# Retention followed by a SoLU layer on one core: another order for the first seven chunks

## The chip, the cores and the metric

The kernel runs on one core of a Trainium2 chip. A core has five engines that run side by side, each with its own queue, in order: PE (matrix multiplication; its weight loads are listed apart as PEld), DVE (vector work), ACT (activation functions and copies with a scale), POOL (a slower vector engine) and SP, which here only issues transfers. The metric is the device time of one execution in microseconds (us), as the median over runs.

## The reference

Two layers follow each other. The first is a retention: scores of queries and keys, scaled, multiplied by a decay that depends on head and distance and is zero above the diagonal, then applied to the values. The second is a dense layer with a softmax in it.

```python
scores = (1 / sqrt(64)) * (q @ k.transpose(0, 1, 3, 2))       # 8 batches, 8 heads, 576 positions, 64 wide
ret = scores * Dmat                                            # gamma[h] ** (i - j) for i >= j, else 0
x = (ret @ v).transpose(0, 2, 1, 3).reshape(4608, 512)
h = x @ w_in                                                   # 512 x 1024
sm = softmax(h)
solu = h * sm
ln = (solu - mean(solu)) / sqrt(var(solu) + 1e-6) * g_ln
out = ln @ w_out                                               # 1024 x 512
```

## The kernel before

The 4608 tokens are cut into 36 chunks of 128. Batches go in pairs: chunk 0 is the first 128 positions of batch 0, chunk 1 those of batch 1, chunk 2 the next 128 of batch 0, and so on through chunk 7; chunk 8 holds the last 64 positions of both. Then the next pair follows. Within a batch a state (keys times values, decayed) is carried from chunk to chunk, so chunk 4 needs the state that chunk 2 has left, and chunk 2 that of chunk 0.

Each chunk passes through a series of small steps, each a function with a name of two letters. In the order of one chunk:

- ld loads q, k and v (three transfers of 256 KB on SP's queue). cq, ck and cv bring them to 16 bits, with the decay factors for q and v.
- tq transposes q and k on PE; eq copies the result out of PSUM (qkT). sc makes the scores on PE; mk multiplies them by the mask on DVE (two instructions).
- kv multiplies keys and values on PE; ad adds the carried state on DVE (t); dk and d3 decay it on POOL in two forms.
- av and fs make the retention's output on PE, from the chunk itself and from the carried state; ex copies it out (xT).
- m1 is the first product of the dense layer, x times w_in (eight matmuls of 512 columns into h); mr is a quarter of it, so that it can start while w_in is still arriving. mx is the row maximum (DVE), xp the exponential (ACT), so the product with h and its sum (DVE), ce the subtraction of the mean (DVE, two instructions), sq the sum of squares (ACT), rt the inverse root (POOL, three instructions).
- tu transposes the result on PE, eu copies it out (uT). m2 is the second product, with w_out (eight matmuls into o). st scales it on ACT and stores it through SP.

Beside these, li loads a quarter of w_in (512 KB) and wi brings half of a quarter to 16 bits; lo loads a quarter of w_out (512 KB) and wo brings an eighth of it to 16 bits with the factor of the norm; wu runs a number of matmuls on a tile of zeros (w), whose result nobody reads; c1 and c2 load and prepare constants. The last letter of a step names its engine where there is a choice: a for ACT, v for DVE, g for POOL.

The order is written out by hand as three strings of such steps, START, LOOP and END, and nothing reorders them: each engine gets its instructions in the order of the string, and each queue its transfers. Waits between engines are set by what is read and written, and by buffers that are used again. `run` (line 612) goes through a string; in LOOP the numbers are relative to the pass, so that pass i makes tu of chunk i-2, so of i-1, m1 and mx of i, kv, ad, av, fs and ex of i+1, tq, eq, sc and mk of i+2 and m2 and st of i-2. START goes as far as pass FIRST, with which the loop begins.

```python
        run(START, 0)
        for i in range(FIRST, NCH - 1):
            run(LOOP, i)
        run(END, NCH - 1)
```

Buffers that matter here: PSUM has four banks of their own for all products but h (tags b0 to b3), and the string BANKS says, allocation by allocation, which of the four is taken; a step that takes a bank waits until what was in it has been read. h has two buffers, released by so. The loads have six buffers of each kind, the 16-bit q, k and v four, uT, u and e three. m2 may not be issued before all eight wo (line 412 ff.).

In START before, SP loads chunk 1, a quarter of w_in, chunk 0, the rest of w_in, chunks 3, 2 and 4, w_out, and then chunks 5 to 9. The first two m2 stand in START, after m1 of chunks 0 to 3, and the loop begins with pass 4.

Of the kernel before, what the change touches and what calls it, by code (L numbers as in the profile page):

```python
# [16 lines left out]

FIRST = 4  # L20
START = """
c1:0 ld:1 li:3 ld:0 ck:0:v li:2 li:1 cq:1:g li:0 cv:1:v ck:1:a cq:0:g wu:0:8 tq:1 ld:3 wu:0:15
kv:1 wi:2:0:v wi:0:0:a eq:1:v ld:2 tq:0 wi:1:1:g cv:0:v wi:3:1:a wu:0:6 sc:1 eq:0:v wi:3:0:a
mk:1 wu:0:3 sc:0 ld:4 kv:0 wi:1:0:v c2:0 lo:0 ad:1 ck:3:a wu:0:1 av:1 ad:0 lo:3 wi:2:1:a mk:0
cq:3:g fs:1 dk:1 tq:3 ex:1:a dk:0 d3:1 wu:0:2 mr:1:3 cq:2:g eq:3:a d3:0 cv:3:v lo:1 mr:1:2
cv:2:g lo:2 ck:2:a wi:0:1:v av:0 kv:3 mr:1:0 sc:3 fs:0 ld:5 cq:4:g ad:3 tq:2 mr:1:1 mk:3
ex:0:a mr:0:2 mr:0:1 kv:2 av:3 mx:1 eq:2:a sc:2 ad:2 dk:3 d3:3 cv:4:g d3:2 mk:2 mr:0:0 mr:0:3
av:2 fs:3 mx:0 fs:2 xp:1 dk:2 wo:0:g ck:4:a ex:2:a tq:4 wo:4:g so:1 kv:4 wu:0:2 m1:2 xp:0
eq:4:a so:0 ce:0 ld:6 wu:0:1 tu:0 ld:7 cq:5:g ce:1 ld:8 ex:3:a ad:4 wo:7:a wo:6:a wo:3:a
wo:2:v sq:1 sc:4 mx:2 m1:3 tu:1 wo:1:a mk:4 eu:0:v av:4 xp:2 wo:5:a ck:5:g cv:5:v tq:5 fs:4  # L30
eq:5:v sq:0 eu:1:a mx:3 rt:1 m2:0 rt:0 cq:6:g so:2 m2:1 st:0 ex:4:a cq:7:g sc:5 ck:6:v cv:6:g
ce:2 xp:3 ld:9 st:1 mk:5 ck:7:g
"""
LOOP = """
tu:-2 so:-1 tq:2 dk:0 d3:0 eq:2:a eu:-2:a ce:-1 m1:0 kv:1 ad:1 av:1 sc:2 mx:0 sq:-2 mk:2 fs:1
# [6 lines left out]
"""  # L42

BANKS = """
012302210201313202132013203200310210302312032103210231023120312032103213021302310231032103213021
302310231032103213021302310231032103201320130213021032103201320130213021032103201320130213021032
10312031201320132103210312031201320132103210312031201320132013231001
"""


# [25 lines left out]
def kernel(  # L76
# [535 lines left out]
    def run(order, base):  # L612

        for token in order.split():
            name, n, *more = token.split(":")
            n = base + int(n)
            if 0 <= n < NCH:
                step[name](n, *more)

    with tc.manual_schedule():  # L620
# [3 lines that stand above are left out]
# [31 lines left out]
```

## Time and profile before

| | us |
|---|---|
| median of 3 runs (lowest, highest) | 227.18 (226.64, 227.31) |
| the profiled execution | 226.83 |
| its span, from the first to the last instruction | 225.0 |
| PE busy in the span (share) | 211.4 (94%) |
| DVE busy | 196.9 (88%) |
| ACT busy | 190.9 (85%) |
| POOL busy | 163.1 (73%) |
| mean granted PE clock | 0.992 |

The page also cuts the span into 40 slices of 5.6 us each and gives the busy share of each in tenths, where 9 is 90% or more:

```
PE   6778889899999999999999999999999999999982
DVE  0078788999999999999999999999999999999780
ACT  2107689699999999999999999999999999999972
```

A busy share is an average over stages with different limits. The start and the last 20 us are filled less than the middle, and a matmul on zeros counts as busy too, so a digit for PE in the first slices says less than one in the middle. What a change is worth is read from the stage where it lies.

### The profile page before, as it was taken

How to read it: one execution, taken by the hardware profiler on the slowest of the kernel's cores; microseconds unless marked ns; L12 is line 12 of the kernel's file. 1: busy time of each engine (PE TensorE's matmuls, PEld its weight loads, DVE VectorE, ACT ScalarE, POOL GpSimd, SP SyncE). 2: the span in 40 equal slices, each digit the busy share in tenths (PEclk: the TensorE clock that was granted, in tenths of full speed). 3: DMA queues.
4: the chain of work that ended last, by engine and by line, in shares of the span. 5: the costliest groups of instructions: out<-in, count | busy, mean ns of one | idle time of the engine just before them, and what ended most of it. 6: DMA issues, size and time to landing. Idle time of an engine off the chain costs nothing.

```text
span 225.0 us, 5803 instructions
## 1 busy us (share of the span) xinstructions
PE 211.4 (94%) x2158; PEld 119.0 (53%) x2158; DVE 196.9 (88%) x340; ACT 190.9 (85%) x299; POOL 163.1 (73%) x243
## 2 busy tenths in 40 slices
PE   6778889899999999999999999999999999999982
PEld 2334355455555555555555555555555555555542
DVE  0078788999999999999999999999999999999780
ACT  2107689699999999999999999999999999999972
POOL 2128868798776998887758989887759988883231
PEclk9699999999999999999999999999999999999999
DMA  7999899999999986988898968988898963111204
GB/s 161 246 345 219 220 332 205 225 235 265 258 216 247 238 165 150 262 198 196 182 215 183 216 134 207 240 203 183 204 197 195 196 136 105 47 50 47 93 3 143
DMA packets 121085, 42.52 MB, mean 189 GB/s; under 512 B 114656, under 2 KB 115040, under 8 KB 121056
## 3 DMA queue, kind: packets, MB, share of 16 engines
q1 hardware_dynamic: 119424, 41.82, 81.4%
q10 hardware_dynamic: 1632, 0.32, 0.9%
q8 instruction: 17, 0.28, 0.5%
q14 instruction: 12, 0.10, 0.2%
HBM read 32.70 MB, written 9.44 MB: 187 GB/s over the span
## 4 chain that ended last, share of the span: by engine, by line
PE 62%; SPq 11%; DVE 10%; ACT 6%; POOL 4%; DMA 4%; issue 2%; ACTq 0%; POOLq 0%; DVEq 0%
PE h L335 20%; PE o L418 20%; SPq L159 9%; PE lp L404 5%; PE tp L189 5%; DMA qf<-in_q_dram 4%; PE sc L213 4%; PE x L303 3%; PE kp L237 3%; PE x L288 3%; ACT e L351 2%; DVE nm L345 2%; SPq L580 2%; DVE u L360 2%; SPq L590 1%
## 5 line engine op out<-in xcount | busy, mean ns | idle before, releaser
L418 PE MATMUL o<-w_out,uT 128*128 128x512 f16 x280 | 66.0, 379 | 0.4
L335 PE MATMUL h<-w_in,xT 128*128 128x512 f16 x264 | 62.4, 379 | 0.1
L166 POOL TENSOR_TENSOR q<-qf,small 128x512 f16<-128x512 f32 x36 | 37.7, 1048 | 12.4 <-DMA qf<-in_q_dram 12.4
L226 DVE TENSOR_TENSOR ret<-sc,tris 128x512 f16<-128x512 f32 x72 | 46.0, 679 | 0.4 <-PE sc L213 0.4
L351 ACT ACTIVATE e<-h,nm 128x1024 f32<-128x1024 f32 x35 | 39.1, 1117 | 6.6 <-DVE nm L345 6.2
L360 DVE SCALAR_TENSOR_TENSOR u<-h,e 128x1024 f16<-128x1024 f32 x35 | 42.4, 1212 | 1.9 <-ACT e L351 1.8
L345 DVE TENSOR_REDUCE nm<-h 128x1 f32<-128x1024 f32 x35 | 42.5, 1214 | 0.9 <-PE h L323 0.9
L418 PEld LDWEIGHTS <-uT 128*128 128x128 f16 x280 | 26.1, 98 | 26.7 <-ACT uT L150 0.7
L383 ACT ACTIVATE sq<-u 128x1024 f16<-128x1024 f16 x35 | 37.4, 1069 | 0.0
L335 PEld LDWEIGHTS <-xT 128*128 128x128 f16 x264 | 24.4, 98 | 23.9 <-issue 0.3
L150 ACT COPY qkT<-tp 128x1024 f16<-128x1024 f16 x33 | 33.4, 1012 | 2.5 <-PE tp L189 1.3
L264 POOL TENSOR_TENSOR s<-t,small 128x512 f16<-128x512 f32 x32 | 33.6, 1053 | 0.0
L150 ACT COPY uT<-lp 128x1024 f16<-128x1024 f16 x33 | 33.6, 1018 | 0.0
L395 POOL TENSOR_TENSOR w<-w,ss 128x1 f32<-128x1 f32 x36 | 6.8, 190 | 34.3 <-ACT sq L383 34.0
L150 POOL CAST k<-kf 128x512 f16<-128x512 f32 x30 | 30.9, 1029 | 0.1
L166 DVE TENSOR_TENSOR v<-vf,small 128x512 f16<-128x512 f32 x33 | 29.3, 887 | 1.8 <-DMA vf<-in_v_dram 1.8
L426 ACT ACTIVATE o_sb<-o,rs 128x512 f32<-128x512 f32 x35 | 23.7, 680 | 0.5 <-POOL rs L396 0.5
L404 PEld LDWEIGHTS <-u 128*128 128x128 f16 x280 | 18.3, 98 | 10.1 <-DVE u L374 1.7
L404 PE MATMUL lp<-ident,u 128*128 128x128 f16 x280 | 21.4, 219 | 1.3 <-ACT o_sb L426 1.0
L150 ACT CAST xT<-x 128x512 f16<-128x512 f32 x36 | 21.1, 586 | 1.1 <-PE x L303 1.0
L396 POOL TENSOR_TENSOR rs<-w,mhalf 128x1 f32<-128x1 f32 x36 | 19.8, 549 | 2.9
L276 POOL TENSOR_TENSOR s<-t,small 128x256 f32<-128x256 f32 x24 | 20.3, 844 | 0.0
(68 smaller groups left out, 255.5 us busy)
## 6 DMA issues: line engine op xcount, KB each, us to landing
qf<-in_q_dram SPq DMA_DIRECT2D x32, 256.0 KB, 4.0
kf<-in_k_dram SPq DMA_DIRECT2D x32, 256.0 KB, 4.6
vf<-in_v_dram SPq DMA_DIRECT2D x32, 256.0 KB, 4.9
out_dram<-o_sb SPq DMA_DIRECT2D x32, 256.0 KB, 2.3
w_in<-in_moe_w_in_dram SPq DMA_DIRECT2D x4, 512.0 KB, 5.8
w_out<-in_moe_w_out_dram SPq DMA_DIRECT2D x4, 512.0 KB, 6.0
qf<-in_q_dram SPq DMA_DIRECT2D x8, 128.0 KB, 3.3
kf<-in_k_dram SPq DMA_DIRECT2D x8, 128.0 KB, 3.3
```

Of the source, the lines that this page charges most:

```text
L150: (engine.copy if engine is nc.scalar else engine.tensor_copy)(out=out, in_=in_)
L166: engine.tensor_tensor(out=dst, in0=T.pop((key, n)), in1=table.unsqueeze(2).to_broadcast([P, H, D]), op=ALU.mult,)
L226: nc.vector.tensor_tensor(out=r, in0=s, in1=m, op=ALU.mult)
L264: nc.gpsimd.tensor_tensor(out=s16, in0=t.unsqueeze(2).to_broadcast([P, 4, 2, D]), in1=gd.unsqueeze(3).to_broadcast([P, 4, 2, D]), op=ALU.mult,
L335: nc.tensor.matmul(out=h[:, i * 512 : (i + 1) * 512], lhsT=xT[:, d], rhs=w_in16[:, d, i * 512 : (i + 1) * 512], start=d == 0, stop=d == 3,)
L345: nc.vector.tensor_reduce(out=nm, in_=T["h", n], axis=AX.X, op=ALU.max, negate=True)
L351: nc.scalar.activation(out=e, in_=T["h", n], func=ACT.Exp, bias=T.pop(("nm", n)), accum_out=s)
L360: nc.vector.scalar_tensor_tensor(out=u, in0=T.pop(("h", n)), scalar=1.0, in1=T.pop(("e", n)), op0=ALU.mult, op1=ALU.mult, accum_out=su,)
L383: nc.scalar.activation(out=s, in_=T.pop(("v", n)), func=ACT.Square, accum_out=ss)
L404: nc.tensor.transpose(out=lp[:, c], in_=u[:, c * P : (c + 1) * P], identity=ident)
L418: nc.tensor.matmul(out=o, lhsT=uT[:, c], rhs=w_out16[:, c], start=c == 0, stop=c == NF - 1)
L426: nc.scalar.activation(out=o_sb, in_=T.pop(("o", n)), func=ACT.Copy, scale=T.pop(("rs", n)))
```

## The change

The change replaces START, moves FIRST from 4 to 7 and rewrites BANKS to fit; no function and no other line is touched. LOOP and END are the same strings, and the loop begins with pass 7.

- SP loads chunks 1 and 0, then all of w_in, then chunks 4, 2, 3, 5 and 6, then w_out, then chunks 7 and up.
- The first products of chunks 0 to 5 stand ahead of the first m2 in the string, and the exponentials of chunks 0, 1, 2 and 4 too (those of 3 and 5 follow it). The m2 of chunks 0, 1, 4, 3 and 2, in this order, come at the end of START, with m1 of chunk 6 among them.
- Up to pass 7 both orders issue the same steps, but for wu: 38 of its matmuls before, 28 after.
- Some steps change engines. To DVE come cq of chunks 0, 1 and 9, eq of chunks 6 to 8, ex of chunks 0 and 6, and eu of chunks 2 and 3; from DVE go, among others, eq of chunks 0, 1 and 5 and eu of chunk 0 (to ACT) and cv of chunks 3, 5, 7 and 9 (to POOL).
- uT is now made for chunks 0, 1 and 4 before the first m2, and for chunks 2 and 3 after it. The stores of chunks 1 and 0 stand on SP's queue ahead of the load of chunk 10, those of chunks 3 and 4 ahead of chunk 11, that of chunk 2 ahead of chunk 12.

```diff
--- before.py
+++ after.py
@@ -17,19 +17,23 @@
 
 
 
-FIRST = 4
+FIRST = 7
 START = """
-c1:0 ld:1 li:3 ld:0 ck:0:v li:2 li:1 cq:1:g li:0 cv:1:v ck:1:a cq:0:g wu:0:8 tq:1 ld:3 wu:0:15
-kv:1 wi:2:0:v wi:0:0:a eq:1:v ld:2 tq:0 wi:1:1:g cv:0:v wi:3:1:a wu:0:6 sc:1 eq:0:v wi:3:0:a
-mk:1 wu:0:3 sc:0 ld:4 kv:0 wi:1:0:v c2:0 lo:0 ad:1 ck:3:a wu:0:1 av:1 ad:0 lo:3 wi:2:1:a mk:0
-cq:3:g fs:1 dk:1 tq:3 ex:1:a dk:0 d3:1 wu:0:2 mr:1:3 cq:2:g eq:3:a d3:0 cv:3:v lo:1 mr:1:2
-cv:2:g lo:2 ck:2:a wi:0:1:v av:0 kv:3 mr:1:0 sc:3 fs:0 ld:5 cq:4:g ad:3 tq:2 mr:1:1 mk:3
-ex:0:a mr:0:2 mr:0:1 kv:2 av:3 mx:1 eq:2:a sc:2 ad:2 dk:3 d3:3 cv:4:g d3:2 mk:2 mr:0:0 mr:0:3
-av:2 fs:3 mx:0 fs:2 xp:1 dk:2 wo:0:g ck:4:a ex:2:a tq:4 wo:4:g so:1 kv:4 wu:0:2 m1:2 xp:0
-eq:4:a so:0 ce:0 ld:6 wu:0:1 tu:0 ld:7 cq:5:g ce:1 ld:8 ex:3:a ad:4 wo:7:a wo:6:a wo:3:a
-wo:2:v sq:1 sc:4 mx:2 m1:3 tu:1 wo:1:a mk:4 eu:0:v av:4 xp:2 wo:5:a ck:5:g cv:5:v tq:5 fs:4
-eq:5:v sq:0 eu:1:a mx:3 rt:1 m2:0 rt:0 cq:6:g so:2 m2:1 st:0 ex:4:a cq:7:g sc:5 ck:6:v cv:6:g
-ce:2 xp:3 ld:9 st:1 mk:5 ck:7:g
+ld:1 c1:0 wu:0:3 ld:0 wu:0:3 cq:1:v li:2 ck:1:v cv:1:v tq:1 li:0 eq:1:a cq:0:v wu:0:5 li:1
+ck:0:a tq:0 eq:0:a wu:0:1 sc:0 li:3 sc:1 wi:2:0:a cv:0:v mk:1 wi:0:1:a mk:0 kv:0 wu:0:2 av:0
+wi:3:0:g c2:0 ld:4 ld:2 kv:1 av:1 wi:0:0:v fs:1 wi:2:1:v wi:3:1:v wi:1:0:g ex:1:a mr:1:3 fs:0
+cq:4:g ad:0 wi:1:1:a ld:3 ex:0:v cq:2:g mr:1:2 ck:4:a mr:0:2 mr:0:3 mr:0:1 mr:1:0 mr:0:0
+cv:4:v tq:4 ad:1 dk:0 d3:6 mx:0 dk:1 mr:1:1 wu:0:3 eq:4:a sc:4 d3:0 ck:2:a mx:1 tq:2 eq:2:a
+xp:0 wu:0:6 sc:2 wu:0:5 mk:4 cv:2:v xp:1 cq:3:g kv:2 ld:5 ck:3:a kv:4 mk:2 ad:2 so:1 av:2 fs:2
+so:0 tq:3 dk:2 av:4 fs:4 ld:6 d3:2 ex:2:a eq:3:a m1:2 cv:3:g kv:3 ce:0 ad:4 ex:4:a ce:1 mx:2
+ck:5:a d3:1 d3:4 sc:3 cq:5:g cv:5:g mk:3 ad:3 sq:1 xp:2 lo:2 dk:4 dk:3 lo:0 cq:6:g ck:6:g m1:4
+tq:5 eq:5:a d3:3 tu:0 sc:5 tu:1 eu:0:a av:3 mx:4 kv:5 cv:6:g lo:3 mk:5 fs:3 av:5 eu:1:a fs:5
+wo:5:g ex:3:a so:2 tq:6 ce:2 ad:5 wo:6:g eq:6:v m1:3 tu:2 ex:5:a sc:6 lo:1 xp:4 wo:0:a so:4
+mk:6 kv:6 ce:4 wo:2:v wo:1:a m1:5 wo:7:a ad:6 dk:6 dk:5 wo:4:a mx:3 av:6 fs:6 tu:4 wo:3:a m2:0
+sq:0 ld:7 xp:3 eu:4:a ck:7:a eu:2:v sq:2 ld:8 m2:1 cq:7:g mx:5 ex:6:v so:3 ce:3 tq:7 m2:4 tu:3
+xp:5 eq:7:v eu:3:v so:5 m1:6 rt:0 ck:8:v sc:7 rt:1 sq:4 rt:2 ld:9 cq:8:g cv:7:g mk:7 st:1 m2:3
+ck:9:v tq:8 m2:2 st:0 mx:6 kv:7 sq:3 eq:8:v rt:4 d3:5 rt:3 ld:10 st:3 cv:9:g av:7 st:4 cq:9:v
+fs:7 ce:5 cq:10:g sc:8 ld:11 st:2 ld:12 ck:10:g ad:7 ex:7:a cv:8:v mk:8 xp:6
 """
 LOOP = """
 tu:-2 so:-1 tq:2 dk:0 d3:0 eq:2:a eu:-2:a ce:-1 m1:0 kv:1 ad:1 av:1 sc:2 mx:0 sq:-2 mk:2 fs:1
@@ -42,9 +46,9 @@
 """
 
 BANKS = """
-012302210201313202132013203200310210302312032103210231023120312032103213021302310231032103213021
-302310231032103213021302310231032103201320130213021032103201320130213021032103201320130213021032
-10312031201320132103210312031201320132103210312031201320132013231001
+012301231010203132013201321031032031203120132132031330230231023103210320132013021302103210320132
+013021302103210320132013021302103210312031201320132103210312031201320132103210312031201320132103
+21023102312031203210321023102312031203210321023102312031203120302112
 """
```

## The prediction

> **What bounds the kernel now.** I read the busy time by stretches first, since it says where an engine is full and where it is not. Columns: the stretch in us, its length, then busy time (and instructions) of PE, PEld, DVE, ACT and POOL, the granted PE clock, the DMA share, GB/s.
>
> ```profile
> 0.00:11.50 11.50, 8.30 (x29) 3.16 (x30) 0.28 (x2) 1.90 (x2) 2.27 (x6) 0.85 1.02 205
> 11.50:25.00 13.50, 10.09 (x112) 5.06 (x111) 10.34 (x18) 5.39 (x10) 7.13 (x9) 1.00 1.15 260
> 25.00:42.84 17.84, 15.92 (x154) 8.29 (x152) 15.76 (x28) 15.68 (x26) 13.34 (x19) 1.00 1.05 262
> 42.84:59.69 16.85, 16.83 (x180) 9.74 (x181) 16.50 (x28) 14.47 (x22) 14.75 (x22) 1.00 1.15 243
> 59.69:204.00 144.31, 144.09 (x1565) 83.98 (x1563) 140.55 (x237) 138.47 (x214) 119.20 (x173) 1.00 0.81 184
> ```
>
> From 59.69 to 204 PE is busy 144.09 of 144.31 us, DVE 140.55 (97%): the loop is bound by PE with DVE close behind, and the work from there on is the same in both kernels. So the change is worth what it moves a **mark** on PE: the start of the transposes of chunk 5 (tu:5), the first instruction of loop pass i=7, where both orders have issued the same set of steps. It is the third line here; DVE's own mark is the start of so:6. (Columns: start us, us, engine line operation.)
>
> ```profile
> 37.66 3.87 PE L418 MATMUL o<-w_out,uT 128*128 128x512 f16 x16
> 42.84 0.62 PE L404 MATMUL lp<-ident,u 128*128 128x128 f16 x8 [0.98 <-ACT o_sb L426]
> 59.69 0.61 PE L404 MATMUL lp<-ident,u 128*128 128x128 f16 x8
> ```
> ```profile
> 45.34 1.19 DVE L374 TENSOR_SCALAR u<-u,nmu 128x1024 f16<-128x1024 f16 x1
> ...
> 49.11 1.14 DVE L166 TENSOR_TENSOR v<-vf,small 128x512 f16<-128x512 f32 x1
> ...
> 60.75 1.21 DVE L360 SCALAR_TENSOR_TENSOR u<-h,e 128x1024 f16<-128x1024 f32 x1
> ```
>
> Up to the mark PE is busy 8.30+10.09+15.92+16.83 = 51.1 us, of which the rows of the warm-up tile w make 12.6 us; some 21 us of 59.69 are idle or warm-up. That is all the change can draw on. What paces this front is the loads:
>
> ```profile
> 23.80 0.62 ACT L150 CAST k<-kf 128x512 f16<-128x512 f32 x1 [2.23 <-DMA kf<-in_k_dram]
> ```
> ```profile
> 34.19 1.04 POOL L605 TENSOR_TENSOR w_out<-w_out,g 128x512 f16<-128x512 f32 x1 [2.27 <-DMA w_out<-in_moe_w_out_dram]
> 35.39 1.04 POOL L166 TENSOR_TENSOR q<-qf,small 128x512 f16<-128x512 f32 x1 [0.17 <-DMA qf<-in_q_dram]
> ```
>
> The keys of chunk 2 are awaited until 23.7, the last piece of w_out until 34.1, and chunk 5, queued behind w_out, until 35.3.
>
> **The loads.** All are on SP's queue and the DMA share is about 1 or more, so I place them by order. Issue plus time to landing, read DMA by DMA, gives before: chunk 1 at 3.9/6.2/7.5 (q/k/v), chunk 0 at 10.3/11.5/12.6, w_in complete 16.6, chunk 3 17.8/19.0/20.2, chunk 2 21.4/23.7/24.6, chunk 4 25.6/26.5/27.7, w_out 34.1, chunk 5 35.3/36.4/38.2, chunk 6 41.3, chunk 7 42.5/43.7/45.3. After, the first fourteen transfers (chunks 1, 0 and w_in) are the same set: w_in at 16.6 again, chunk 0 some 1.5 earlier. Chunk 4 takes the place of 3 (20.2), 2 stays (24.6), 3 takes that of 4 (27.7). Then 5 and 6 at 1.2 a transfer: 31.3 and 34.9; w_out at 1.6 a piece (before, four in 27.7 to 34.1): 41.3; chunk 7 at the old time. Stores queue on SP too: ld:10 now stands behind st:1 and st:0 (about 52), so q of chunk 10 lands near 57. It is first read by POOL as START ends and transposed a pass later (about 64): I cost it at nothing; without that cover it is 1 us a us.
>
> **The early part.** The h of chunks 0 and 1 needs all of w_in (16.6) plus a POOL cast (0.78): 17.4. Sixteen matmuls at 1.73/8 = 0.216 make 3.5, so DVE's first maximum starts near 21.5, against 25.34. Little of these 4 us survives: DVE runs mx:0, mx:1 (1.14 each), mk:4 (1.2), cv:2 (0.62) and then stands at mk:2. That needs k of chunk 2 at 23.7, the cast 0.62, transposes 0.45 and 0.16 of tail (379 less 216 ns), ACT's copy 1.0 beside six warm-ups, scores 0.33: mask at 26.4, 27.6 after it; ad:2 to 28.15.
>
> **DVE from there** (start to start, from the rows of before): so 6 x 1.25, ce 6 x 0.59, ad 5 x 0.35, mx 5 x 1.14, mk 5 x 1.20, eq 3 x 0.60, eu 2 x 0.60, wo 0.40, ex 0.60, ck 2 x 0.34, cq and cv 0.62 each = 30.4 us up to so:6. The reorder gives DVE more than it had (eq:6 to eq:8, ex:6, eu:2, eu:3, against eq:5 and eu:0 before), which takes time from ACT, and here it is DVE that is full. Two waits are built in. eu:2 is the fourth uT of a pool of three (chunks 0, 1, 4 come first), so it waits for m2:0 to end. m2:0 starts at 44.15 (below) and takes 1.73 plus tail: 46.1, with DVE ready at 45.0: 1.1 us. Behind eu:2 stand mx:5, ex:6, so:3 and all after. eu:3 waits for tu:3, whose bank is freed by the eq:7 just ahead of it: 0.65. So so:6 starts at 28.15+30.4+1.75 = 60.3 at best (60.75 before). PE's tu:5 reuses the bank of kv:7 that ad:7 empties, and after ad:7 DVE has cv:8 and mk:8 (1.8): mark 58.5.
>
> The traced stretches are longer than such a sum. From 25.34 to 60.75 before, 35.4 us, the same addition gives 32.2 and the waits 1.5: 1.7 are stretched rows (the 1.19 and 1.14 above, for 0.49 and 0.68). For the new order I take 1.1 in 32 us, ends 0 and 1.7. Mark: 59.6, **0.1 earlier**.
>
> **PE and the banks.** At the loop's spacing (tq 0.45, sc 0.33, kv 0.15, av 0.32, fs 0.23, h 1.82, tu 0.45, o 1.73; 9, 9, 8, 8, 6, 7, 5 and 5 of them) the steps to the mark are 35.8 us of PE, 7.5 of them done by 28.0: 28.3 left, so PE alone could be there at 56.3. That bounds the gain at 3.4. Each of four banks is handed back by a copy: sc:8 waits for st:2, that for m2:2, that (bank of sc:7) for mk:7; these fit inside DVE's 55 to 59, so no further cost. Ten fewer warm-ups (38 to 28) save nothing: they filled waits.
>
> **w_out behind chunk 6.** ACT ends xp:2 at 34.4, then eq:5, eu:0, eu:1 (0.91 each), ex:3 and ex:5 (0.5 each, the second behind fs:5 at 38.1) and xp:4 (1.1): its five conversions run from 39.7 to 42.8 (0.62 each). DVE's steps sum to wo:2 at 43.1 and ad:6 at 43.8; m2:0, which takes the bank that ad:6 empties, stands behind tu:4 at 44.15. With 41.3 the load has 1.8 us of cover at wo:2; beyond that a late us costs a us.
>
> **Handover.** DVE trails PE by 60.75-59.69 = 1.06 before, 1.8 after. In a pass m2 starts 3.7 after the transposes (57.96 and 54.21) and needs ad, done 2.4 after so: a lag of 1.3 is free. Chunk 8 has no ad (0.35 less DVE), so 0 to 0.3; I take 0. Sum: 226.83 (profiled, span 225.0) less 0.1 = 226.7. That execution lies 0.35 under the median 227.18; set against the median, **227.0**.
>
> [...] With PE busy 0.63 of 2.66 us the granted clock fell and stayed down 3.3 us:
>
> ```profile
> 4.50:7.16 2.66, 0.63 (x9) 0.46 (x9) 0.00 (x0) 0.62 (x1) 0.57 (x1) 1.00 1.31 218
> 7.50:10.80 3.30, 3.30 (x10) 1.21 (x8) 0.00 (x0) 0.00 (x0) 0.44 (x1) 0.50 1.28 255
> ```
>
> Up to w_in's arrival the new order holds 14 warm-ups (3, 3, 5, 1, 2) where the old one had 33 by 18.1 us, and leaves PE mostly idle from 9 to 17.4. [...]
>
> **Rivals.**
> - *Faster, 0.31.* The rows do not stretch (mark 58.5, -1.2), or the two DVE waits shrink too, down to PE's own 56.3 (-3.4). For: stretching was 0.2 of 1.7 before 42.8. Against: POOL is as busy as before. Taken -1.7: 225.5.
> - *Slower: w_out late, 0.20.* SP was held up in issuing single transfers for 2.7 to 4.5 us (vf of chunk 5: 4.54, for about 1.2 usual). Two such holds ahead of w_out land it near 45, past 43.1; DVE stands at wo:2, all later steps with it: +2, 229.1. Against: the holds of 2.7 to 3.3 before 24 us are already in the landings used above.
> - *Cold PE at h of chunks 0 and 1, 0.15.* Warm-ups in the first stretch ran 8 in 3.33 us, 0.42 each; at that price for 10 of the 14 matmuls ahead of mx:0 (the low clock's 3.3 us hold 8, a late start of it 13) the maximum comes 10 x 0.204 = 2.0 us later; 0.8 of that lies in DVE's wait for chunk 2 (ready 25.6, mask 26.4). +1.2: 228.2. It decides once mx:0 is later than 22.3.
>
> **Numbers.** Forecast 0.34, its own range 226.3 to 227.9 (stretch 0.4 to 1.7, lag 0 to 0.3). A measurement here tells 0.3%, 0.7 us, from nothing. Faster: 0.31 + 0.06 of the forecast's lower end = 0.37. Same: 0.21 + 0.02 of the cold case = 0.23. Slower: 0.07 + 0.20 + 0.13 = 0.40. Range 225.1 to 229.3: it cuts the rare deep gain and double delays.
>
> **What would show it.** Right: the first maximum near 21.5; mk:2 at 26 to 27; the last w_out piece at 41 to 42; the first o matmul near 44; from there PE nearly full; tu:5 at 59 to 60 with DVE's so:6 1.5 to 2 us behind; no other change up to the end. Wrong: tu:5 before 58.5 or after 60.5, a granted clock of 0.5 after 18, DVE idle at wo:2, or a loop that is no longer PE end to end.

## The result and the profile after

The changed kernel takes 228.36 us (median of 5 runs, 228.14 to 229.39) against 227.02 (226.64 to 227.31) for the kernel before: a ratio of 1.0069, 95% interval 1.0043 to 1.0095 (the two medians alone give 1.0059). It is slower by 1.3 us; the forecast was no change at 227.0. The profiled execution took 228.14 with a span of 226.4, against 226.83 and 225.0. One execution further down, of the version with w_out ahead of chunk 5, took 306.98 us at a mean clock of 0.659, and its ratio leaves it out.

The busy time in the same five stretches, columns as in the prediction:

```profile
0.00:11.50 11.50, 6.80 (x28) 2.50 (x28) 3.07 (x7) 3.00 (x4) 0.19 (x4) 0.82 1.06 198
11.50:25.00 13.50, 11.17 (x94) 5.77 (x94) 8.53 (x14) 5.41 (x8) 6.19 (x8) 0.65 1.18 271
25.00:42.84 17.84, 16.57 (x209) 10.05 (x207) 17.66 (x32) 15.69 (x25) 14.50 (x16) 1.00 1.12 264
42.84:59.69 16.85, 15.94 (x129) 8.16 (x128) 14.83 (x27) 11.93 (x21) 13.74 (x24) 1.00 0.87 200
59.69:204.00 144.31, 143.90 (x1557) 83.91 (x1556) 140.69 (x239) 138.73 (x213) 117.95 (x172) 1.00 0.82 188
```

Two columns matter. The granted PE clock (third from the end) is 0.65 in the second stretch, where it was 1.00. DVE is full in the third (17.66 of 17.84 us, 15.76 before), as the reorder gives it more work; in the fourth it is less busy than before (14.83 us for 16.50), mostly for the two waits of 1.18 and 0.70 us that the prediction had built in. The last row is the loop, as full as it was. PE's mark, and the two groups of matmuls that matter ahead of it (start us, us, engine line operation, idle before it and what ended that):

```profile
17.99 4.70 PE L327 MATMUL h<-w_in,xT 128*128 128x512 f16 x14 [0.68 <-ACT xT L154]
...
45.38 1.89 PE L422 MATMUL o<-w_out,uT 128*128 128x512 f16 x8
...
60.36 0.61 PE L408 MATMUL lp<-ident,u 128*128 128x128 f16 x8 [0.25 <-DVE t L256]
```

The h of chunks 0 and 1 starts 0.6 later than it should (18.0 for 17.4), and its 14 matmuls take 4.70 us, 0.336 each where the sum had 0.216. The mark, tu:5, is at 60.36: 0.67 later than before (59.69), and 0.8 later than forecast. On DVE:

```profile
20.02 0.69 DVE L170 TENSOR_TENSOR v<-vf,small 128x512 f16<-128x512 f32 x1 [1.64 <-DMA vf<-in_v_dram]
...
22.73 2.36 DVE L349 TENSOR_REDUCE nm<-h 128x1 f32<-128x1024 f32 x2 [1.68 <-PE h L327]
25.01 1.28 DVE L230 TENSOR_TENSOR ret<-sc,tris 128x512 f16<-128x512 f32 x2
26.20 1.02 DVE L170 TENSOR_TENSOR v<-vf,small 128x512 f16<-128x512 f32 x1
27.14 1.28 DVE L230 TENSOR_TENSOR ret<-sc,tris 128x512 f16<-128x512 f32 x2
...
47.31 0.69 DVE L154 COPY uT<-lp 128x1024 f16<-128x1024 f16 x1 [1.18 <-PE o L422]
...
62.03 1.21 DVE L364 SCALAR_TENSOR_TENSOR u<-h,e 128x1024 f16<-128x1024 f32 x1
```

DVE stands 1.68 us for that h; its first maximum (mx:0) starts at 22.73, and the mask of chunk 2 (mk:2), the last line before a stretch without gaps, at 27.14. The built-in wait at eu:2 is there (1.18, the row at 47.31). So:6 starts at 62.03, 1.28 later than before.

Behind the mark nothing is new: the last matmul of the second product starts 0.59 later than before (219.68 against 219.09). The rest of the 1.4 us between the two spans lies in the last stores and did not come again: from the mark to the end of the span it is 165.3 before, 166.0 in this trace and 165.4 to 165.5 in all nine later traces of the new order and its variants.

PE's clock in two-us windows shows where it was lost. The kernel after:

```profile
10.00:12.00 2.00, 1.26 (x8) 0.45 (x5) 0.69 (x1) 1.21 (x2) 0.00 (x0) 0.50 1.05 359
12.00:14.00 2.00, 1.03 (x16) 0.89 (x17) 0.45 (x1) 1.27 (x3) 0.00 (x0) 0.50 1.03 412
...
18.00:20.00 2.00, 2.00 (x5) 0.72 (x6) 0.38 (x1) 1.07 (x2) 1.12 (x2) 0.50 1.36 218
20.00:22.00 2.00, 2.00 (x8) 0.84 (x7) 1.03 (x2) 0.00 (x0) 0.72 (x1) 0.73 1.36 222
```

The kernel before:

```profile
12.00:14.00 2.00, 1.65 (x22) 1.11 (x21) 0.64 (x2) 0.00 (x0) 0.00 (x0) 1.00 0.99 385
14.00:16.00 2.00, 1.16 (x12) 0.47 (x11) 2.00 (x4) 0.00 (x0) 0.78 (x2) 1.00 1.08 369
```

After, the clock is at 0.50 from about 7.5 to 21.1 us, although PE is busy half of the time or more; before, it was low for some 3.4 us (7.5 to 10.9) and then stayed up.

### The profile page after: what moved, and what is told of

It is laid out like the page before. It is cut to its first block, busy times and chain, and to the rows that moved or that the text cites. A ratio compares the mean times of both kernels' runs of the same rounds, so it can differ in the third digit from the quotient of the medians.

```text
span 226.4 us, 5767 instructions
## 1 busy us (share of the span) xinstructions
PE 211.1 (93%) x2148; PEld 119.5 (53%) x2148; DVE 198.7 (88%) x345; ACT 190.3 (84%) x297; POOL 159.0 (70%) x240
## 4 chain that ended last, share of the span: by engine, by line
PE 71%; DVE 12%; ACT 6%; DMA 5%; issue 2%; SPq 1%; POOL 0%; ACTq 0%; DVEq 0%; POOLq 0%
PE h L339 21%; PE o L422 20%; PE tp L193 6%; PE lp L408 5%; PE sc L217 5%; PE x L292 3%; PE x L307 3%; PE kp L241 3%; DMA kf<-in_k_dram 3%; DVE u L364 3%; DVE ret L230 2%; PE h L327 2%; DVE nm L349 2%; DMA vf<-in_v_dram 2%; PE w L562 2%
## 5 line engine op out<-in xcount | busy, mean ns | idle before, releaser
L154 ACT COPY qkT<-tp 128x1024 f16<-128x1024 f16 x33 | 33.4, 1012 | 9.5 <-PE tp L193 8.4
L268 POOL TENSOR_TENSOR s<-t,small 128x512 f16<-128x512 f32 x32 | 33.5, 1052 | 5.7 <-DVE t L256 5.7
L170 POOL TENSOR_TENSOR q<-qf,small 128x512 f16<-128x512 f32 x33 | 34.6, 1050 | 2.9 <-DMA qf<-in_q_dram 2.9
L154 ACT COPY uT<-lp 128x1024 f16<-128x1024 f16 x32 | 32.5, 1016 | 0.1
L399 POOL TENSOR_TENSOR w<-w,ss 128x1 f32<-128x1 f32 x36 | 6.9, 192 | 33.9 <-ACT sq L387 33.4
L170 DVE TENSOR_TENSOR v<-vf,small 128x512 f16<-128x512 f32 x31 | 26.4, 852 | 4.1 <-DMA vf<-in_v_dram 4.1
L154 POOL CAST k<-kf 128x512 f16<-128x512 f32 x27 | 28.5, 1055 | 0.0
L430 ACT ACTIVATE o_sb<-o,rs 128x512 f32<-128x512 f32 x35 | 23.5, 681 | 3.5 <-PE o L422 2.6
L154 ACT CAST xT<-x 128x512 f16<-128x512 f32 x34 | 19.9, 586 | 3.4 <-PE x L292 3.0
```

What stands on the lines that cost most here:

```text
L154: (engine.copy if engine is nc.scalar else engine.tensor_copy)(out=out, in_=in_)
L170: engine.tensor_tensor(out=dst, in0=T.pop((key, n)), in1=table.unsqueeze(2).to_broadcast([P, H, D]), op=ALU.mult,)
L268: nc.gpsimd.tensor_tensor(out=s16, in0=t.unsqueeze(2).to_broadcast([P, 4, 2, D]), in1=gd.unsqueeze(3).to_broadcast([P, 4, 2, D]), op=ALU.mult,
L430: nc.scalar.activation(out=o_sb, in_=T.pop(("o", n)), func=ACT.Copy, scale=T.pop(("rs", n)))
```

## The experiments

All start from the changed kernel unless said otherwise. The theory after the result: the low clock makes h late, and the mask of chunk 2 with it. The rivals: DVE's own load and its wait at eu:2 set the time whatever the clock; or one execution's trace misleads.

**The changed kernel again**, unchanged, for its spread.

> The new order once more, unchanged, for a second trace of it. In the first trace the granted clock was 0.50 from about 7.5 to 21.4 us, the 14 matmuls of h ahead of mx:0 took 4.70 us, tu:5 (the mark) began at 60.36 (59.69 before) and the last 5.9 us of the order before had become 6.7. If the low clock is what makes the kernel slower, the mark moves with it: 60.3 to 60.4 where the clock is low again, 59.6 to 59.7 where it is not, and the time with it by 0.7. If the clock has no part, the mark is 60.3 whatever the clock shows. If the longer end (0.8) belongs to one execution and not to the order, it is between 5.8 and 6.9 here, and need not be 6.7.

Measured: 228.19 us against 226.89, ratio 1.0050 (1.0032 to 1.0069): slower again. Its profiled execution is a milder one, with the clock low only from about 13.1 to 20 us (0.79 in 12 to 14, 0.50 in 14 to 20). PE, then DVE:

```profile
17.28 4.50 PE L327 MATMUL h<-w_in,xT 128*128 128x512 f16 x14 [0.69 <-POOL w_in L154]
```
```profile
21.82 2.36 DVE L349 TENSOR_REDUCE nm<-h 128x1 f32<-128x1024 f32 x2 [0.85 <-PE h L327]
...
26.30 1.29 DVE L230 TENSOR_TENSOR ret<-sc,tris 128x512 f16<-128x512 f32 x2 [0.33 <-PE sc L217]
```

H is slow here too, but began 0.7 earlier; DVE then still waits 0.33 for the scores of chunk 2, so the low clock costs nothing behind mk:2 (26.30), and the mark is at 59.81, not at the 60.3 that both theories expected under a low clock. The spans of this kernel's 11 executions go from 225.2 to 226.5 (median 226.0; 225.1 for the kernel before). What the low clock costs thus differs from execution to execution.

**More warm-ups**: the same order, with four groups enlarged, so that 29 instead of 14 warm-ups stand ahead of h (2163 matmuls in all, 2148 after; the text below says 12 more, its groups make 15).

```diff
-... wu:0:3 ld:0 wu:0:3 ... cq:0:v wu:0:5 li:1 ... eq:0:a wu:0:1 sc:0 ... kv:0 wu:0:2 av:0
+... wu:0:3 ld:0 wu:0:10 ... cq:0:v wu:0:6 li:1 ... eq:0:a wu:0:4 sc:0 ... kv:0 wu:0:6 av:0
```

> The new order with 12 more warm-up matmuls in places where PE waits: 10 for 3 in the second step, 6 for 5 after tq:1, 4 for 1 after tq:0, 6 for 2 after kv:0. Clock theory: the clock is up when h of chunks 0 and 1 begins (18.0), its 14 matmuls take 3.0 us in place of 4.7, mx:0 starts at 21.0 to 21.5 in place of 22.7, mk:2 at 26.3 to 26.6 in place of 27.1, and the mark is 0.5 to 0.7 earlier: ratio to before 1.003 to 1.004 in place of 1.007. Rival (DVE's own load sets the mark, the early part is hidden by the wait for chunk 2): mx:0 is earlier but the mark stays at 60.2 to 60.5, ratio 1.006 to 1.008. A third outcome, the warm-ups themselves in the way: mx:0 not earlier.

Measured: 227.10, ratio 1.0012 (0.9997 to 1.0027): no longer told from the kernel before, and 1.09 us under the changed kernel in the same set of runs. Its trace, PE and then DVE:

```profile
17.59 3.18 PE L327 MATMUL h<-w_in,xT 128*128 128x512 f16 x14 [0.99 <-POOL w_in L154]
...
59.67 0.61 PE L408 MATMUL lp<-ident,u 128*128 128x128 f16 x8 [0.39 <-DVE t L256]
```
```profile
21.08 0.69 DVE L170 TENSOR_TENSOR v<-vf,small 128x512 f16<-128x512 f32 x1 [3.08 <-DMA vf<-in_v_dram]
...
22.03 2.34 DVE L349 TENSOR_REDUCE nm<-h 128x1 f32<-128x1024 f32 x2
...
26.31 1.28 DVE L230 TENSOR_TENSOR ret<-sc,tris 128x512 f16<-128x512 f32 x2
```

H is back to 0.227 a matmul, the clock reads 1.00 throughout, mk:2 is at 26.31 and the mark at 59.67 (the forecast had 59.6). DVE's first maximum is then held by the values of chunk 4, not by PE. Five of its 12 executions still show a mean clock of 0.985 and spans of 225.7 to 226.1, against 225.0 to 225.4 for the other seven at 0.998 or more: within one kernel, too, the low clock goes with the longer span. Of the 1.09 us, the median spans account for 0.7 (226.0 to 225.3). The remainder lies outside the span: around it are 1.75 to 1.84 us in all twelve executions here, but 2.57 to 2.82 in four of the eleven of the unchanged kernel. No trace shows what that is, or that the clock has a part in it.

**A fourth buffer for uT**, with the few warm-ups and with the many. This takes away what eu:2 waits for.

```diff
-    utp = ctx.enter_context(tc.tile_pool(name="utp", bufs=3))
+    utp = ctx.enter_context(tc.tile_pool(name="utp", bufs=4))
```

> The new order with four uT buffers in place of three, nothing else. eu:2, the fourth, need no longer wait for the end of the first m2 (DVE stood there 1.18 us, PE 0.78 us behind it). If DVE's chain sets the mark, eu:2 begins at 46.1 in place of 47.3 and the mark and so:6 come 1.0 to 1.2 earlier: mark 59.2 to 59.4, ratio to before 1.001 to 1.003. If PE and the banks set it (sc:8 behind st:2 behind m2:2), the wait moves to the next step (eu:3 or mk:7) and the mark comes 0 to 0.4 earlier, ratio 1.005 to 1.007.

> Both edits, warm-ups and the fourth uT buffer. If both costs lie on one chain of DVE they add: mark 58.5 to 58.8 (0.9 to 1.2 ahead of the order before), ratio to before 0.996 to 0.999. If they hide each other (one chain ends where the other does), the mark is no earlier than the better one alone, 59.2 or later, ratio 1.001 to 1.004.

Measured: 228.35, ratio 1.0057 (1.0037 to 1.0076), with few warm-ups; 226.93, ratio 1.0000 (0.9986 to 1.0015), with many. The wait is gone in both traces, and hardly anything came of it: from mk:2 to the mark it is 33.4 us with few and 33.2 with many; in the three traces with three buffers it is 33.2, 33.5 and 33.4. With many warm-ups so:5 starts 1.13 us earlier (51.54, 52.67 with three buffers), but so:6 only 0.10 earlier (61.24, 61.34). DVE between the two, with four buffers:

```profile
52.68 0.75 DVE L154 CAST k<-kf 128x512 f16<-128x512 f32 x1
...
54.55 0.78 DVE L154 CAST k<-kf 128x512 f16<-128x512 f32 x1
...
58.02 1.08 DVE L378 TENSOR_SCALAR u<-u,nmu 128x1024 f16<-128x1024 f16 x1
```

and POOL at the same time:

```profile
52.11 1.04 POOL L170 TENSOR_TENSOR v<-vf,small 128x512 f16<-128x512 f32 x1
...
54.44 0.61 POOL L280 TENSOR_TENSOR s<-t,small 128x256 f32<-128x256 f32 x1
...
57.34 1.49 POOL L170 TENSOR_TENSOR q<-qf,small 128x512 f16<-128x512 f32 x1
```

Each of these DVE rows began while the POOL row ran, and ended 0.27 to 0.28 us behind it (53.43 and 53.15; 55.33 and 55.05; 59.10 and 58.83). With three buffers they took 0.42, 0.42 and 0.65. That is 0.33 + 0.36 + 0.43 more; with cv:8 0.08 more and cq:9 0.18 less it makes 1.02 of the 1.03 us that went. What stretched them no trace shows, and not every overlap did: with three buffers the cast at 53.81 also began under a POOL row (from 53.46, 0.80 us) and took 0.42.

**A new trap in the same trace.** With few warm-ups and four buffers h is the slowest of this set, while the clock column reads 1.00. PE's row and the window around it:

```profile
18.16 5.20 PE L327 MATMUL h<-w_in,xT 128*128 128x512 f16 x14 [0.68 <-ACT xT L154]
```
```profile
16.00:20.00 4.00, 3.32 (x30) 1.84 (x30) 2.55 (x6) 1.72 (x3) 2.57 (x4) 1.00 1.36 222
```

0.371 a matmul cannot be the full clock that gave 0.227 above, and four transposes take 0.61 at 9.8 and 10.9, as under 0.50 in the first trace (0.39 or 0.40 at full clock): here the column is wrong and the spacing of the matmuls right. Mx:0 is at 23.39, mk:2 at 27.51, the mark at 60.87.

**Hardly any warm-up**: every group of the changed kernel cut to one matmul (eight groups, so 8 matmuls for 28; the text below says ten).

> The new order with each of its ten groups of warm-ups cut to one matmul (10 in place of 28). Clock theory: PE is at half clock in nearly every execution when h of chunks 0 and 1 begins, its 14 matmuls take 5 to 6 us, mx:0 starts at 23.4 to 24.4, mk:2 at 27.5 to 28.5, the mark at 60.8 to 61.8; ratio 1.007 to 1.011, above that of the new order (1.005 to 1.007). If warm-ups only cost PE time (11 of them stand between tq:2 and kv:2), the mark is earlier: 59 to 60, ratio 0.999 to 1.003.

Measured, in four executions: 229.65, ratio 1.0137 (1.0118 to 1.0157), above the 1.007 to 1.011 expected.

```profile
18.28 5.13 PE L327 MATMUL h<-w_in,xT 128*128 128x512 f16 x14 [0.68 <-ACT xT L154]
...
31.57 2.35 PE L339 MATMUL h<-w_in,xT 128*128 128x512 f16 x8
```

H takes 5.13 us, mx:0 starts at 23.45, mk:2 at 27.52 and tu:5 at 62.42. Up to mk:2 this is as with few warm-ups and four buffers; a further 1.5 us is lost behind it, where the groups of 6 and 5 warm-ups around the scores of chunk 2 are missing too. One such place is the first product of chunk 2, which takes 2.35 us for 1.89 and starts at 31.57 for 30.19 in the changed kernel; the transposes ahead of it take 0.63 us there (29.61 and 30.03), 0.39 in the changed kernel.

**The kernel before with few warm-ups**: its own order, with the first five groups cut from 33 to 15.

```diff
-... cq:0:g wu:0:8 tq:1 ld:3 wu:0:15 ... cv:0:v wi:3:1:a wu:0:6 sc:1 ... mk:1 wu:0:3 sc:0
+... cq:0:g wu:0:6 tq:1 ld:3 wu:0:5 ... cv:0:v wi:3:1:a wu:0:1 sc:1 ... mk:1 wu:0:2 sc:0
```

> The order before with the warm-ups that the new order has up to w_in's arrival: 6, 5, 1, 2, 1 in place of 8, 15, 6, 3, 1. If the old order owes its time to its warm-ups as the new one does, h of chunks 0 and 1 runs at 0.34 to 0.43 a matmul from 20.7 and mx:1 starts at 26 to 27 in place of 25.3: mark 60.2 to 61.2, ratio 1.003 to 1.008. If its waits (DVE waited 0.9 for that h, and 1.05 for v of chunk 5 at 38.3, whatever came first) take the delay in, mark 59.6 to 59.8, ratio 0.999 to 1.001.

Measured: 226.95, ratio 1.0017 (0.9998 to 1.0037): not told from no change. H is slow at its start here too. Before, PE and then DVE:

```profile
20.71 1.04 PE L323 MATMUL h<-w_in,xT 128*128 128x512 f16 x4 [0.17 <-ACT xT L150]
```
```profile
25.34 1.22 DVE L345 TENSOR_REDUCE nm<-h 128x1 f32<-128x1024 f32 x1 [0.93 <-PE h L323]
...
38.27 0.72 DVE L166 TENSOR_TENSOR v<-vf,small 128x512 f16<-128x512 f32 x1 [1.05 <-DMA vf<-in_v_dram]
```

With few warm-ups:

```profile
21.64 1.40 PE L323 MATMUL h<-w_in,xT 128*128 128x512 f16 x4
```
```profile
25.61 1.21 DVE L345 TENSOR_REDUCE nm<-h 128x1 f32<-128x1024 f32 x1
...
39.77 0.69 DVE L166 TENSOR_TENSOR v<-vf,small 128x512 f16<-128x512 f32 x1 [2.43 <-DMA vf<-in_v_dram]
```

The old order has cover at the step that waits for h: DVE stood there 0.93 us before and not at all now, so its first maximum (mx:1) is only 0.27 later, and the mask of chunk 2 0.08 later (27.08 for 27.00). The mark of this trace is late all the same (60.91, the span 226.2), but for another reason: DVE waits for the values of chunk 5, which land 1.5 us later, after the last piece of w_out ahead of them landed 1.2 later; whether that is chance, one trace does not say. Other executions of the same kernel have spans from 224.4 on (median 225.1, 225.0 before).

**w_out ahead of chunk 5**, with many warm-ups: the other placement that the change could have chosen.

```diff
-... kv:2 ld:5 ... lo:2 ... lo:0 ... lo:3 ... lo:1 ...
+... kv:2 lo:2 lo:0 lo:3 lo:1 ld:5 ...
```

> The new order with the 12 warm-ups, and w_out's four loads moved ahead of chunk 5 (so behind five chunks, as in the order before). If w_out behind chunk 6 is a gain of the new order, chunk 5 lands 6.4 us later (its v near 38), mk:5 moves from 36.0 to 38.5 and the mark with it, 59.7 to about 62: ratio 1.010 to 1.014. If w_out's late arrival costs the new order time (first m2 at 44.6), its conversions come earlier and the mark with them, 59.0 to 59.6: ratio 0.997 to 1.001.

Measured: 231.71 to 233.04 us in four executions, ratio 1.0258 (1.0235 to 1.0280), the mark at 65.07. The direction was expected, the size was not: 5.4 us at the mark where some 2.5 were thought of. DVE waits for the scores of chunk 5, whose load now stands behind 2 MB:

```profile
40.97 1.29 DVE L216 TENSOR_TENSOR ret<-sc,tris 128x512 f16<-128x512 f32 x2 [4.97 <-PE sc L203]
```

**Less work on DVE** at the end of START, with many warm-ups and four buffers: k of chunks 8 and 9 and eq of chunk 8 go to ACT, q of chunk 9 to POOL, and a few steps move.

```diff
-xp:5 eq:7:v eu:3:v so:5 m1:6 rt:0 ck:8:v sc:7 rt:1 ... st:1 m2:3
-ck:9:v tq:8 m2:2 st:0 mx:6 kv:7 sq:3 eq:8:v rt:4 d3:5 rt:3 ld:10 st:3 cv:9:g av:7 st:4 cq:9:v
-fs:7 ce:5 cq:10:g sc:8 ld:11 st:2 ld:12 ck:10:g ad:7 ex:7:a cv:8:v mk:8 xp:6
+xp:5 eq:7:v eu:3:v so:5 m1:6 rt:0 sc:7 rt:1 ... st:1 st:0 ck:8:a
+m2:3 tq:8 m2:2 mx:6 kv:7 sq:3 ck:9:a rt:4 rt:3 d3:5 ld:10 st:3 st:4 eq:8:a cv:9:g av:7 cq:9:g fs:7
+ce:5 cv:8:v cq:10:g sc:8 ld:11 st:2 ld:12 ck:10:g ad:7 ex:7:a mk:8 xp:6
```

> Warm-ups and four uT buffers as in the run before, and at the end of START five steps taken off DVE: ck:8, ck:9 and eq:8 to ACT (which stood idle 2.6 to 2.9 us ahead of st:3), cq:9 to POOL, cv:8 moved ahead of ad:7 into its wait, and rt:3 ahead of d3:5. About 2 us less DVE up to so:6. If DVE's load late in START sets the mark (its steps between SBUF tiles ran 0.33 to 0.43 longer each beside POOL in the run before), tu:5 comes at 58.6 to 58.9 in place of 59.5, so:6 at 59.6 to 60.0 in place of 61.2, and the ratio to before is 0.995 to 0.997. If the banks set it (sc:8 behind st:2 behind m2:2), tu:5 stays at 59.2 to 59.5 and the ratio at 0.999 to 1.001.

Measured: 225.82, ratio 0.9965 (0.9947 to 0.9982): faster than both kernels. The four steps that left DVE took 3.15 us there (0.75, 0.78, 0.68, 0.94), but from mk:2 to the mark only 0.9 was won (32.3 for 33.2; 32.5 and 32.6 in the next two traces). PE is next, and ahead of the mark it stands 0.51 us itself, for ACT's copy of eq:8, one of the steps that were moved there. PE, then DVE:

```profile
58.42 0.41 PE L292 MATMUL x<-ret,v 128*64 128x128 f16 x8 [0.51 <-ACT qkT L154]
```
```profile
59.52 1.29 DVE L230 TENSOR_TENSOR ret<-sc,tris 128x512 f16<-128x512 f32 x2 [0.72 <-PE sc L217]
```

Even with 29 warm-ups ahead of h, 3 of its 12 executions, the profiled one among them, show a mean clock of 0.981 and spans of 224.7 to 224.9, against 223.7 to 224.3 for the others.

**The same with 36 warm-ups ahead of h, and with 14.** The order of this kernel stays; only the groups change (3, 10, 10, 5, 8, and the 3, 3, 5, 1, 2 of the changed kernel).

> The version that beats both, with seven more warm-ups (10 for 6 after tq:1, 5 for 4 after tq:0, 8 for 6 after kv:0). There 3 of 12 executions still showed a mean clock of 0.981 and a span of 224.7 to 224.9, against 223.7 to 224.3 of the others. Clock theory: such executions become rarer or vanish, the median falls to 225.5 to 225.8, ratio to before 0.994 to 0.996. Rival (the warm-ups are now in the way: at half clock ten of them last 4.3 us and hold the transposes of chunk 0 back): no fewer, or the short spans themselves grow by 0.3 or more, ratio 0.997 to 0.999.

> The same version with the warm-ups of the new order (3, 3, 5, 1, 2). If the low clock is a cost of its own it comes back in full: 0.9 to 1.3 us more than with the 12 warm-ups, ratio 1.000 to 1.003. If the lighter DVE takes the late start of mk:2 in, the ratio stays at 0.996 to 0.998.

Measured: 225.81, ratio 0.9958 (0.9944 to 0.9971), with 36; 227.45, ratio 1.0034 (1.0019 to 1.0050), with 14. The h ahead of mx:0 with 36, then with 14:

```profile
17.50 3.19 PE L327 MATMUL h<-w_in,xT 128*128 128x512 f16 x14 [0.68 <-ACT xT L154]
```
```profile
17.39 4.68 PE L327 MATMUL h<-w_in,xT 128*128 128x512 f16 x14 [0.68 <-POOL w_in L154]
```

Between 14 and 29 or 36 lie 1.6 us (227.45 to 225.82 and 225.81), more than the 0.9 to 1.3 expected; 1.4 of it lies in the median spans (225.4 to 224.0). Seven more on top of 29 do not move the median, but 11 of 12 spans are now within 223.8 to 224.4. With 36, mk:2 is at 26.22 and the mark at 58.73. By its ratio the version with 36 is 0.42% faster than the kernel before, not told from the one with 29 (0.35%).

## Why the prediction was wrong, step by step

- **The loads** held: the values of chunk 4 were there by 20.0 (20.2 forecast), and no step stood for w_out: ACT's last conversion ended at 43.8, and DVE's wo:2 began at 44.2 without a wait.
- **The step that failed**: "Sixteen matmuls at 1.73/8 = 0.216 make 3.5, so DVE's first maximum starts near 21.5", and with it "Ten fewer warm-ups (38 to 28) save nothing: they filled waits". They filled waits; but in the trace with 29 ahead of h the clock reads 1.00 throughout, in the profiled execution with 14 it was 0.50 from 7.5 to 21.1 us. With 14 ahead of h a matmul took 0.336 (0.371 in another execution) and the first maximum started at 22.73 (23.39), the mask of chunk 2 at 27.14 where 26.4 was forecast, and that 0.7 is what the mark lost. The sign of being wrong that the prediction named, a granted clock of 0.5 after 18, was there. Adding 15 back, with nothing else touched, gave 0.227 and took away 1.09 of the 1.30 us lost in that set of runs; 0.7 of this is span, and why the rest lies outside it no run shows. (The sum itself slips without harm: 17.4 and 3.5 make 20.9, not 21.5, and only fourteen of the sixteen matmuls stand ahead of mx:0.)
- **The rival was there** with its mechanism: cold PE at h, deciding "once mx:0 is later than 22.3". Where mx:0 is late, mk:2 comes 4.1 us or more after it (23.39 to 27.51; 23.45 to 27.52; 22.73 to 27.14), and in no trace before 26.15, so the point is 22.2 or a little less. Its price of +1.2 fits the trace in which mx:0 was as late as it had it (23.39 for 23.5): the mark at 60.87, 1.3 behind the forecast's 59.6. In the profiled execution mx:0 was only at 22.73 and the mark 0.8 behind; that its time comes near the rival's 228.2 even so is partly luck, as 0.7 us of it lies in the last stores. The 13 matmuls at low clock of a late start, which with the 8 gave it 10, no run shows: in the profiled execution the 14 took 4.70 us, where 29 warm-ups gave 3.18, so 1.5 us more for the 2.0 it had. Its chance, 0.15, was too low: of the 0.40 that the prediction gave to a slower kernel, 0.20 hung on a late w_out, which did not come. The evidence stood in the prediction's own fence: after PE had been busy 0.63 of 2.66 us the old clock read 0.50 for 3.3 us, and the new order was said to leave PE "mostly idle from 9 to 17.4"; one low spell of 3.3 us was then assumed over by the time of h. It lasted 13.6 us in the profiled execution.
- **DVE from there** held closely: from so:1 (28.69) to so:6 (62.03) it took 33.34 us, where 30.4 + 1.75 + 1.1 = 33.25 were forecast, with 1.18 and 0.70 for the two waits. DVE bound this part, as argued.
- **The gain that was hoped for** is not there even at full clock: the first maximum comes at 22.0 instead of 25.3, but the loads (mk:2 is not before 26.2) and DVE's longer list use up the 3.3 us, and the mark is at 59.67 for 59.69. That is the forecast's own sum, and the run with 15 more warm-ups confirms it (ratio 1.0012).
- **The handover** cost nothing, as taken: the last second product moved by 0.59 for 0.67 at the mark.
- "DVE idle at wo:2", the sign of a late w_out, did not show; and of the two places for w_out that were run, the one behind chunk 6 is better by 2.5% for this START.

What stays open: why the clock stays low with PE busy 1.0 to 1.6 of each 2 us (after, 8 to 16 us) and stays up with 1.2 to 1.7 (before, 12 to 20); why the values of chunk 4 land at 21.0 to 21.2 in four of the five traces with many warm-ups and at 20.0 to 20.2 with few; and what the up to 1 us outside the span is.

## What to carry to other kernels

A matmul on zeros that fills a wait is work with a purpose: before it is dropped or costed at nothing, look at which real matmuls come next, and what they cost at the low clock (those of h took 0.32 to 0.37 us each with 14 warm-ups ahead of them, 0.23 with 29 or 36). Price it at the step that waits for them, with the cover that this step has; here half a per cent hung on 15 of them. And taking away a wait on a full engine is worth little while the same engine's later rows, stretched beside POOL (0.33 to 0.43 us each here), or the engine next in line take the time back: take load off it as well, and expect the next engine to cap the gain (0.6 to 0.9 of 3.15 us here).

## What the runs showed that was not expected

- The granted clock in a row can read 1.00 while the matmuls under it are 0.35 to 0.37 us apart (0.23 to 0.26 at full clock); it did so at the start of three of the traces (few warm-ups with four buffers, hardly any, and the kernel before with few). The spacing of equal matmuls is the better witness.
- One kernel's low clock is not one cost: with 14 warm-ups the spans of one kernel ran from 225.2 to 226.5 and of another from 224.2 to 226.0. The 15 warm-ups are worth 1.09 of 228 us, or 0.5%, and that parts a slower kernel (ratio 1.0050) from one not told from the kernel before (1.0012); with hardly any warm-up the kernel is 1.2% slower than with 29 (ratios 1.0137 and 1.0012).
- With four buffers and many warm-ups two DVE casts took 0.75 and 0.78 us, and a tensor_scalar 1.08, where they took 0.42 and 0.65 with three; each started under a POOL instruction and ended 0.27 to 0.28 us after it. The row of 1.19 us that the prediction showed as stretched fits too: it ends at 46.53, a POOL instruction that it began under at 46.25.
